# The first piece of w_down in three loads instead of one: 112, 12 and 4 partitions

## The chip, the cores and the metric

The kernel runs on one core of one Trainium2 chip. The metric is the device time of one execution in microseconds (us); the number compared is the median of several runs. A core has five engines that run their own instruction streams: PE (TensorE, matrix multiplications; its weight loads are counted apart as PEld), DVE (VectorE), ACT (ScalarE), POOL (GpSimd) and SP (SyncE, which here only issues loads). Sixteen DMA engines move data between the chip's memory (HBM) and the on-chip buffer of 128 partitions.

## What is computed

One token for each of two batch rows goes through a transformer block with adaptive layer norm: a modulation vector from the condition `c`, attention over a window of cached keys and values, and a gated feed-forward network. Cut to what matters:

```python
mod = (silu(c) @ w_mod).reshape(2, 6, 1, 640)          # sa, ca, ga, sb, cb, gb
h = layernorm(x) * (1 + ca) + sa
q = h @ wq                                             # 32 heads of 192
k, v = k_cache[:, :, -1024:, :], v_cache[:, :, -1024:, :]
o = softmax(q @ k.T * 192**-0.5) @ v
x = x + ga * (o.reshape(2, 1, 6144) @ wo)
h = layernorm(x) * (1 + cb) + sb
x = x + gb * ((gelu(h @ w_gate) * (h @ w_up)) @ w_down)   # 640 -> 1536 -> 640
```

All inputs are bf16. `w_down` has 1536 x 640 elements.

## The kernel before

Everything that is large comes from HBM once, by loads that SP issues: w_mod, wq, the nine pieces of the keys and values, wo, w_gate, w_up and w_down, in this order, 76.9 MB in all. They land in one large buffer, `arena` (L194), whose places are used again: the table `place` (L198 to L215) says at which columns each piece stands, and its order is the order of issue. The function `pump` (L333) issues the next loads as far as the pieces that stood in the same columns have been consumed; SP then waits for PE's counter where it must. All loads are issued by the line L290 (`k_dma`), so it is one line in the profile. Each load has a semaphore of its own (`sem_of`, L286), which is raised sixteen times in all while it lands, and whoever reads the piece waits for 16.

The kernel keeps track of who writes and reads what by keys: a piece is cut into units of 128 columns, each one key (`keys`, L300), and `_Sched` (L29) works out from them which waits an instruction needs.

w_down is laid out with 12 rows of the matrix on each partition, (p r) n -> p (r n), and comes as three pieces, `WD_SPLIT` (L172): the rows 0 to 7 of each partition, 10,240 B a partition (1280 KB in all), then the rows 8 to 10 (480 KB), then row 11 (160 KB). `source` (L311) gives the place in HBM and `view` (L306) the place in `arena`; both take all 128 partitions. They are the last three loads of the kernel.

On the compute side, DVE multiplies a piece of the keys by the query (L512), PE sums it over groups (L524), DVE sums the rest (L531); the softmax follows (L536 to L555), and PE multiplies the weights with the values (L575). After the last values come the output projection (L634), the second layer norm, w_gate and w_up (L655), and the product of both halves, which DVE transposes to `aT` (L669). Then PE multiplies by w_down in three groups of matmuls (L677), one for each piece of `WD_SPLIT`: 64, 24 and 8 matmuls, all added up in one PSUM bank. Each group waits for `aT` and for its own piece. Two DVE steps (L683, L685) and the store on ACT's queue (L687) end the kernel. ACT's queue also loads `c` (2 rows) and x (8 rows) at the start (L346, L347). PE fills its waits with matmuls whose result is not used (`keep_clock`).

Of the kernel before, what the change touches and what calls it, by code (L numbers as in the profile page):

```python
# [119 lines left out]
def bass_adaLN_cond__sliding_block_cached__geglu_ffn__decode_kernel(  # L120
# [14 lines left out]
    P = 128  # L135
    B, _, D = A_x.shape
    _, H, Sk, Dh = A_k_cache.shape
# [12 lines left out]
    FC = F // P  # L150
# [13 lines left out]
    UNIT = 128  # L164
# [5 lines left out]
    WO_SPLIT = [(0, NT)]  # L170
    WU_SPLIT = [(0, KT)]
    WD_SPLIT = [(0, 8), (8, 3), (11, 1)]  # L172
    RB = 16
    RM = RB * (B - 1) + 1
    SB = RB // 2
    OC = DR // 2
    GM = SB + 1
    OM = RB + SB + 1
    ZW = P + DD - 1
# [8 lines left out]
    with es:  # L188
        S = _Sched(nc, es)
# [4 lines left out]
        arena = sb("arena", [P, NAR], BF16)  # L194
# [3 lines left out]
        place = {("wm", 0): (0, KT * 6 * D), ("wq", 0): (4 * HS, wq_n[0])}  # L198
        tiles = [("k", 0, 0, 10), ("k", 0, 1, 12), ("k", 0, 2, 0), ("v", 0, 0, 5), ("k", 1, 0, 9), ("v", 0, 1, 0), ("k", 1, 1, 5), ("v", 1, 0, 9), ("v", 1, 1, 0)]
        span = {}  # L200
        for kind, b, t, z in tiles:
            j0, n = (K_SPLIT if kind == "k" else V_SPLIT)[b][t]
# [7 lines left out]
        o_d = o_u + KT * F  # L210
        place[("wg", 0)] = (o_g, KT * F)
        for i, (k0, nk) in enumerate(WU_SPLIT):
            place[("wu", i)] = (o_u + k0 * F, nk * F)
        for i, (r0, nr) in enumerate(WD_SPLIT):
            place[("wd", i)] = (o_d + r0 * D, nr * D)  # L215
        assert all(o % UNIT == 0 and n % UNIT == 0 and o + n <= NAR for o, n in place.values())
        wm_v = arena[:, 0:KT * 6 * D].rearrange("p (k n) -> p k n", k=KT)
        wg_v = arena[:, o_g:o_g + KT * F].rearrange("p (k n) -> p k n", k=KT)
# [46 lines left out]
        aR = sb("aR", [P, FT], BF16)  # L265
        aT = sb("aT", [P, RB + FC * 32], BF16)
        halfsel = sb("halfsel", [P, 2], F32)
# [8 lines left out]
        BK_OT = 6  # L276
# [4 lines left out]
        def bank(k):  # L281
            return ("bank", k)

        sem_x = S.sem("d_x")
        sem_c = S.sem("d_c")
        sem_of = {it: S.sem("d_%s" % "_".join(str(z) for z in it)) for it in place}  # L286
        sem_out = S.sem("d_out")

        def k_dma(dst, src):
            return lambda e: e.dma_start(dst, src)  # L290
# [3 lines left out]
        queue = {"next": 0, "done": set(), "ops": {}}  # L294

        def overlap(x, y):
            (a, m), (b, n) = place[x], place[y]
            return a < b + n and b < a + m

        def keys(it, lo=0, width=None):  # L300
            o, n = place[it]
            width = n - lo if width is None else width
            assert lo + width <= n
            return [("ar", z) for z in range((o + lo) // UNIT, -(-(o + lo + width) // UNIT))]

        def view(it, lo=0, width=None):  # L306
            o, n = place[it]
            width = n - lo if width is None else width
            return arena[:, o + lo:o + lo + width]

        def source(it):  # L311
            kind = it[0]
            if kind == "wm":
                return w_mod.rearrange("(p k) n -> p (k n)", k=KT)
            if kind == "wq":
                k0, n = WQ_SPLIT[it[1]]
                return A_wq.rearrange("(p k) n -> p (k n)", k=KT)[:, k0 * NQ:(k0 + n) * NQ]
            if kind == "wo":
                t0, n = WO_SPLIT[it[1]]
                return A_wo.rearrange("(p t) n -> p (t n)", t=NT)[:, t0 * D:(t0 + n) * D]  # L320
            if kind == "wg":
                return B_w_gate.rearrange("(p k) n -> p (k n)", k=KT)
            if kind == "wu":
                k0, nk = WU_SPLIT[it[1]]
                return B_w_up.rearrange("(p k) n -> p (k n)", k=KT)[:, k0 * F:(k0 + nk) * F]
            if kind == "wd":
                r0, nr = WD_SPLIT[it[1]]
                return B_w_down.rearrange("(p r) n -> p (r n)", r=FC)[:, r0 * D:(r0 + nr) * D]
            b, (j0, n) = it[1], span[it]
            src = A_k_cache if kind == "k" else A_v_cache  # L330
            return src[b][:, K0:Sk, :].rearrange("h (x j) d -> h x j d", x=XQ)[:, :, j0:j0 + n, :].rearrange("h x j d -> h x (j d)")

        def pump(*consumed):  # L333
            queue["done"].update(consumed)
            while queue["next"] < len(items):
                n = queue["next"]
                it = items[n]
                if not all(x in queue["done"] for x in items[:n] if overlap(x, it)):
                    break
                queue["ops"][it] = S.dma("sp", k_dma(view(it), source(it)), sem_of[it], writes=keys(it), name="ld_%s" % "_".join(str(z) for z in it))  # L340
                queue["next"] += 1

        pump()
        wm_dma = queue["ops"][("wm", 0)]
        S.op("pool", lambda e: e.memset(xr[:, :], 0.0), writes=["xr"], name="xr0")
        S.dma("act", k_dma(crow[:, :], c[:, :]), sem_c, writes=["crow"], name="ld_c")  # L346
        S.dma("act", k_dma(xr[0:P:RB, :], A_x[:, 0, :].rearrange("b (i n) -> i b n", i=NR)), sem_x, writes=["xr"], name="ld_x")  # L347
        S.op("pool", lambda e: e.memset(epsc[:, 0:1], 0.0), writes=["epsc"], name="epsc0")
        S.op("pool", lambda e: e.memset(epsc[:, 1:2], EPS), reads=["epsc"], writes=["epsc"], name="epsc1")
        for nm, t in (("scT", scT), ("oT", oT)):  # L350
# [6 lines left out]
             reads=["ones_f"], writes=["ident_f"], name="ident_f")  # L357
        S.op("pool", lambda e: e.tensor_copy(out=ident_b[:, :], in_=ident_f[:, :]),
             reads=["ident_f"], writes=["ident_b"], name="ident_b")
        S.op("pool", lambda e: e.memset(aT[:, 0:RB], 0.0), writes=["aT0"], name="aT0")  # L360
        S.op("pool", lambda e: e.memset(selq[:, :, :], 0.0), writes=["selq"], name="selq0")
        for b in range(B):
# [4 lines left out]
                 reads=["ones_b"], writes=[("selt", b)], name="selt%d" % b)  # L367
            S.op("pool", lambda e, b=b: e.tensor_copy(out=selq[:, b, :].rearrange("p (u x) -> p u x", x=SQW)[:, :, 0:P].rearrange("p u (i v) -> p u i v", i=NR)[:, :, :, 0:XQ],
                                                      in_=selt[:, b, :].rearrange("p (i x) -> p i x", x=XQ).unsqueeze(1).broadcast_to([P, HB, NR, XQ])),
                 reads=[("selt", b), "selq"], writes=["selq"], name="selq%d" % b)  # L370
        S.op("pool", lambda e: e.memset(scl[:, :], SCALE), writes=["scl"], name="scl")
        S.op("pool", lambda e: e.memset(zsel[:, :, :], 0.0), writes=["zsel"], name="zsel0")
        for i in range(2):
            S.op("pool", lambda e, i=i: e.affine_select(out=zsel[:, :, :], in_=zsel[:, :, :], pattern=[[-P, 2], [-1, ZW]],
                                                        compare_op=ALU.not_equal, fill=1.0, base=DD - 1 - 2 * P * i, channel_multiplier=DD),
                 reads=["zsel"], writes=["zsel"], name="zsel%d" % (i + 1))
# [4 lines left out]
             reads=["ident_f"], writes=["mask_h"], name="mask_h")  # L381
        S.op("dve", lambda e: e.tensor_reduce(out=st32[:, :], in_=ident_f[:, :].rearrange("p (i m) -> p m i", m=32), axis=AX.X, op=ALU.add),
             reads=["ident_f"], writes=["st32"], name="st32")
        S.op("dve", lambda e: e.tensor_reduce(out=halfsel[:, :], in_=st32[:, :].rearrange("p (h m) -> p h m", h=2), axis=AX.X, op=ALU.add),
             reads=["st32"], writes=["halfsel"], name="halfsel")
# [3 lines left out]
             reads=["st32"], writes=["selstat"], name="selstat")  # L389
# [3 lines left out]
        def c_T(e):  # L393
            last = None
            for j in range(KT):
# [4 lines left out]
             reads=[bank(BK_T)], writes=["scT"], name="silu")  # L400
        S.op("dve", lambda e: e.tensor_copy(out=X[:, :], in_=xr[:, :]),  # L401
             reads=["xr"], writes=["X"], name="x_f32")
# [26 lines left out]
        def ln_mod(tag, opc_idx, s_idx, dst_bf):  # L429
# [15 lines left out]
             reads=["mask_h"], writes=["maskc"], name="maskc")  # L445
        S.op("dve", lambda e: e.tensor_copy(out=maskE[:, :], in_=mask_h[:, :]), reads=["mask_h"], writes=["maskE"], name="maskE")

        for half in range(2):
            def f(e, half=half):
                last = None  # L450
                for k in range(KT):
# [9 lines left out]
                 reads=[bank(half)], writes=[("modR", half)], name="mod%d_evac" % half)  # L461
            S.op("dve", lambda e, half=half: e.tensor_scalar(out=opc[:, half, :], in0=modR[:, 3 * half + 1, :], scalar1=1.0, scalar2=None, op0=ALU.add),  # L462
                 reads=[("modR", half)], writes=[("opc", half)], name="opc%d" % half)
# [27 lines left out]
        for n in range(NQB):  # L491
            if n % 2 == 0:
                S.op("act", lambda e, n=n: e.activation(out=qrow[:, n * QW:(n + 1) * QW], in_=ps[:, n, :], func=ACTF.Copy),  # L493
                     reads=[bank(n)], writes=[("qrow", n)], name="q1_evac%d" % n)
            else:
                S.op("dve", lambda e, n=n: e.tensor_copy(out=qrow[:, n * QW:(n + 1) * QW], in_=ps[:, n, :]),  # L496
                     reads=[bank(n)], writes=[("qrow", n)], name="q1_evac%d" % n)
        for b in range(B):
            def f(e, b=b):
                last = None  # L500
                for u in range(HB):
# [5 lines left out]
                 reads=[bank(BK_T + b)], writes=[("qbc", b)], name="q2_evac%d" % b)  # L507
# [78 lines left out]
        for n, it in enumerate(tiles):  # L586
            kind, b, t = it
# [7 lines left out]
            j0, w = span[it]  # L595
# [16 lines left out]
        def p_sel(e):  # L612
            last = None
            for dd in range(DD):
# [10 lines left out]
             reads=[bank(BK_OT), "oT"], writes=["oT"], name="oT")  # L625
# [3 lines left out]
        def wo_f(e):  # L629
            last = None  # L630
            wv = view(("wo", 0)).rearrange("p (t i n) -> p t i n", t=NT, i=NR)
            for t in range(NT):
# [9 lines left out]
             reads=[bank(2), ("modR", 0)], writes=["lnt"], name="ga_attn")  # L642
        S.op("dve", lambda e: e.tensor_tensor(out=X[:, :], in0=lnt[:, :], in1=X[:, :], op=ALU.add),
             reads=["lnt", "X"], writes=["X"], name="x1")
# [4 lines left out]
        def ffn_gu(bk, wv, name, splits):  # L649
            for ci, (k0, nk, key) in enumerate(splits):  # L650
# [12 lines left out]
             reads=[bank(0)], writes=["gl"], name="gelu")  # L663
# [4 lines left out]
             reads=[bank(1), "gl"], writes=["aR"], name="geglu")  # L668
        S.op("dve", lambda e: e.transpose(aT[:, RB:RB + FC * 32], aR[:, :]), reads=["aR"], writes=["aT"], name="aT")  # L669
        for ci, (r0, nr) in enumerate(WD_SPLIT):  # L670
            def f(e, r0=r0, nr=nr):
                last = None
                for fc in range(r0, r0 + nr):
                    wv = wd_v[:, fc, :].rearrange("p (i h n) -> p i h n", i=NR, h=2)
                    for h, a, m in ((1, 0, OM), (0, RB, GM)):
                        for i in range(NR):
                            last = e.matmul(ps[32 * i:32 * i + m, BK_OT, CY:CY + OC], lhsT=aT[:, 32 * fc + a:32 * fc + a + m], rhs=wv[:, i, h, :],  # L677
                                            start=(fc == WD_SPLIT[0][0] and h == 1), stop=(fc == WD_SPLIT[-1][0] and h == 0), tile_position=(0, 32 * i),
                                            skip_group_check=True)
                return last  # L680
            S.op("pe", f, reads=["aT", "aT0"] + keys(("wd", ci)), writes=[bank(BK_OT)], name="down%d" % ci)

        S.op("dve", lambda e: e.tensor_tensor(out=fin[:, :], in0=ps[:, BK_OT, CY:CY + OC], in1=go[:, :], op=ALU.mult),  # L683
             reads=[bank(BK_OT), "go"], writes=["fin"], name="gb_y")
        S.op("dve", lambda e: e.tensor_tensor(out=finb[:, :], in0=fin[:, :], in1=xo[:, :], op=ALU.add),  # L685
             reads=["fin", "xo"], writes=["finb"], name="outR")
        S.dma("act", k_dma(out[:, 0, :].rearrange("b (u n) -> u b n", n=OC), finb[0:P:SB, :]),  # L687
              sem_out, reads=["finb"], name="st_out")
# [17 lines left out]
        for n, x in enumerate(body):  # L706
            if x.opcode != "Matmult":
                continue
            w = x.ins[1]
# [37 lines left out]
```

## Time and profile before

| | us |
|---|---|
| median of 3 runs | 185.89 (185.77 to 185.96) |
| the profiled execution | 185.71 |
| its span, first to last instruction | 184.5 |
| read from HBM | 76.88 MB, 417 GB/s over the span |
| w_up, issue to landing | 23.0 |
| w_down, first, second, third piece, issue to landing | 25.8, 26.4, 26.4 |
| last load issued | 155.4 |
| first, second, third group of w_down's matmuls start | 180.39, 181.43, 181.84 |

The profile is of one execution. It gives the busy time of each engine, the span in 40 equal slices (each digit is a busy share in tenths), the DMA queues (q1 is SP's, q10 ACT's; q8 and q14 carry instructions and tables), the chain of waits that ended last (each line: start, length, what), groups of instructions by source line, and a timeline. The busy times count no instructions that only wait or issue. Behind these views the trace has a record of each DMA packet (queue, start, length, bytes, but not which of the sixteen engines) and the time of each semaphore increment.

### The profile page before, as it was taken

The numbers are of one execution on the slowest core, as the hardware profiler recorded it, in microseconds if no ns is written. First come the engines' busy times: TensorE is split into PE (matmuls) and PEld (weight loads), VectorE is DVE, ScalarE is ACT, GpSimd is POOL, SyncE is SP. The second block draws the span as 40 slices with busy tenths as digits, with TensorE's granted clock in tenths as the row PEclk, the third lists the DMA queues.
The fourth block names the chain that finished last, engine by engine and source line by source line (L and its number), as shares of the span: only waits on it lengthen the run. The fifth ranks groups of instructions, "written<-read, shape, count | busy, mean of one in ns | idle before, by whom it ended". The sixth has DMA issues, their size and how long they took to land.

```text
span 184.5 us, 1871 instructions
## 1 busy us (share of the span) xinstructions
PE 107.9 (59%) x967; PEld 28.2 (15%) x695; DVE 107.2 (58%) x105; ACT 14.4 (8%) x27; POOL 6.1 (3%) x23
## 2 busy tenths in 40 slices
PE   0017000966665095653599565957663299898783
PEld 0012000130000000002351000600000266405212
DVE  6022200039994499964991999587995658300631
ACT  2042000042000000001000000010000100320410
POOL 8400000000000000000000000000000000000000
PEclk9999755599999669997569999988999579999999
DMA  8999997999898989899999989898989999989991
GB/s 292 492 483 440 426 426 330 448 442 494 368 490 362 501 352 512 362 481 416 437 458 409 469 373 480 384 480 373 490 373 480 426 453 470 426 340 400 418 393 46
DMA packets 2495, 76.99 MB, mean 417 GB/s; under 512 B 310, under 2 KB 440, under 8 KB 568
## 3 DMA queue, kind: packets, MB, share of 16 engines
q1 hardware_dynamic: 2448, 76.87, 97.1%
q8 instruction: 6, 0.10, 0.2%
q10 hardware_dynamic: 40, 0.01, 0.0%
q14 instruction: 1, 0.01, 0.0%
HBM read 76.88 MB, written 0.00 MB: 417 GB/s over the span
## 4 chain that ended last, share of the span: by engine, by line
DMA 58%; DVE 22%; PE 17%; ACT 1%; issue 1%; SPq 0%
DMA arena<-in_A_k_cache_dram 36%; DMA arena<-in_B_w_down_dram 14%; DVE arena L512 12%; PE ps L575 8%; DMA arena<-in_w_mod_dram 8%; DVE S_sb L531 6%; PE ps L524 5%; DVE Em L561 2%; PE ps L454 2%; DVE negm L541 1%; ACT E_sb L549 1%; PE ps L552 1%; PE ps L545 1%; DVE M L537 0%; SPq L290 0%
## 5 line engine op out<-in xcount | busy, mean ns | idle before, releaser
L524 PE MATMUL ps<-arena,ident_b 128*128 128x512 bf16 x192 | 49.3, 400 | 28.4 <-DVE arena L512 28.3
L512 DVE TENSOR_TENSOR arena<-arena,qbc 128x3072 bf16<-128x3072 bf16 x32 | 54.8, 1750 | 9.2 <-DMA arena<-in_A_k_cache_dram 7.5
L575 PE MATMUL ps<-arena,Em 128*64 128x384 bf16 x256 | 25.5, 367 | 5.6 <-DVE Em L561 5.6
L531 DVE TENSOR_REDUCE S_sb<-ps 128x32 f32<-128x1024 f32 x16 | 19.5, 1219 | 8.5 <-PE ps L524 8.5
L575 PEld LDWEIGHTS ps<-arena,Em 128*64 128x64 bf16 x256 | 15.9, 124 | 30.4 <-DVE Em L561 22.2
L561 DVE TENSOR_TENSOR Em<-E_sb,maskE 128x2048 bf16<-128x2048 bf16 x8 | 18.0, 2283 | 2.3 <-PE ps L575 2.3
L486 PE MATMUL ps<-arena,hT 128*2 128x512 bf16 x60 | 5.9, 573 | 14.7 <-DMA arena<-in_A_wq_dram 14.7
L496 DVE CAST qrow<-ps 128x512 bf16<-128x512 f32 x1 | 0.7, 691 | 18.7 <-PE ps L486 18.7
L408 PE MATMUL ps<-Em,ident_b 128*128 128x512 bf16 x48 | 11.2, 379 | 0.4 <-issue 0.3
L539 PEld LDWEIGHTS ps<-ident_f,M 128*1 128x1 f32 x2 | 0.2, 80 | 61.0 <-DVE M L537 61.0
L641 DVE TENSOR_TENSOR lnt<-ps,modR 128x160 f32<-128x160 f32 x1 | 0.3, 325 | 12.9 <-PE ps L634 12.9
L549 ACT ACTIVATE E_sb<-S_sb,nbias 128x256 bf16<-128x256 f32 x2 | 1.0, 508 | 66.3 <-DVE nbias L547 66.3
L582 ACT ACTIVATE On<-ps,rden 128x384 bf16<-128x384 f32 x2 | 1.2, 580 | 48.6 <-PE ps L575 48.6
L454 PE MATMUL ps<-arena,scT 128*17 128x480 bf16 x40 | 3.5, 523 | 1.9 <-DMA arena<-in_w_mod_dram 1.9
L634 PEld LDWEIGHTS ps<-arena,oT 128*17 128x17 bf16 x192 | 3.3, 91 | 7.6 <-DMA arena<-in_A_wo_dram 7.6
L396 PE MATMUL ps<-ident_b,crow 2*128 2x2 bf16 x5 | 0.4, 177 | 6.6 <-DMA crow<-in_c_dram 6.6
L634 PE MATMUL ps<-arena,oT 128*17 128x160 bf16 x192 | 3.5, 233 | 0.8 <-DMA arena<-in_A_wo_dram 0.8
L417 PE MATMUL ps<-st,selstat 128*128 128x2 f32 x4 | 0.9, 298 | 4.9 <-ACT sqj L413 4.9
L401 DVE CAST X<-xr 128x160 f32<-128x160 bf16 x1 | 0.2, 244 | 6.0 <-DMA xr<-in_A_x_dram 6.0
L486 PEld LDWEIGHTS ps<-arena,hT 128*2 128x2 bf16 x20 | 0.7, 118 | 19.2 <-issue 19.2
L462 DVE TENSOR_SCALAR opc<-modR 128x160 f32<-128x160 f32 x2 | 0.4, 223 | 4.1 <-ACT modR L459 4.1
L493 ACT ACTIVATE qrow<-ps 128x512 bf16<-128x512 f32 x2 | 1.1, 594 | 19.9 <-PE ps L486 19.9
(86 smaller groups left out, 51.4 us busy)
## 6 DMA issues: line engine op xcount, KB each, us to landing
arena<-in_A_v_cache_dram SPq DMA_DIRECT2D x4, 6144.0 KB, 26.5
arena<-in_A_k_cache_dram SPq DMA_DIRECT2D x3, 6144.0 KB, 36.9
arena<-in_A_wq_dram SPq DMA_DIRECT2D x1, 7680.0 KB, 31.5
arena<-in_A_wo_dram SPq DMA_DIRECT2D x1, 7680.0 KB, 27.7
arena<-in_A_k_cache_dram SPq DMA_DIRECT2D x2, 3072.0 KB, 42.3
arena<-in_w_mod_dram SPq DMA_DIRECT2D x1, 4800.0 KB, 14.2
arena<-in_B_w_gate_dram SPq DMA_DIRECT2D x1, 1920.0 KB, 21.0
arena<-in_B_w_up_dram SPq DMA_DIRECT2D x1, 1920.0 KB, 23.0
```

The source lines that it names most:

```text
L408: last = e.matmul(ps[:, BK_T, :], lhsT=ident_b[:, :], rhs=Em[:, 0, 0:512 // H, :].rearrange("p j h -> p (j h)"), start=True, stop=True)
L454: last = e.matmul(ps[32 * i:32 * i + RM, half, 0:MH].rearrange("p (m n) -> p m n", n=DR), lhsT=scT[:, k, :], rhs=wv[:, 3 * half:3 * half + ...
L486: last = e.matmul(ps[32 * i:32 * i + B, n, :], lhsT=hT[:, k, 0:RM:RB], rhs=wv[:, kk, i, n * QW:(n + 1) * QW], start=(k == 0), stop=(k == K ...
L512: S.op("dve", lambda e: e.tensor_tensor(out=kt, in0=kt, in1=qbc[:, b, :].unsqueeze(1).broadcast_to([P, JC, Dh]), op=ALU.mult), reads=[("qb ...
L524: last = e.matmul(o_ap, lhsT=ident_b[:, :], rhs=kt[:, :, t * GC:(t + 1) * GC], start=(t == 0), stop=(t == NCH - 1))
L531: S.op("dve", lambda e: e.tensor_reduce(out=S_sb[:, b, 2 * JC * pair:2 * JC * (pair + 1)], in_=ps[:, 2 * z:2 * z + 2, :].rearrange("p k (j ...
L541: S.op("dve", lambda e: e.tensor_reduce(out=negm[:, b, :].rearrange("p (h x) -> p h x", x=XQ), in_=ps[0:1, BK_T, 0:P].rearrange("p (h x) - ...
L545: S.op("pe", lambda e: e.matmul(ps[:, BK_T, P:P + 1], lhsT=negm[:, b, :], rhs=scl[:, :], start=True, stop=True), reads=[("negm", b), "scl" ...
L549: S.op("act", lambda e: e.activation(out=E_sb[:, b, :], in_=S_sb[:, b, :], func=ACTF.Exp, scale=SCALE, bias=nbias[:, b:b + 1], accum_out=d ...
L561: S.op("dve", lambda e, z=z, j=j: e.tensor_tensor(out=Em[:, z, :, :], in0=E_sb[:, b, j:j + JE].unsqueeze(2).broadcast_to([P, JE, H]), in1= ...
L575: last = e.matmul(ps[64 * i:64 * i + 2 * H, BK_O, 0:ON], lhsT=Em[:, z, 2 * jp:2 * jp + 2, :].rearrange("p j h -> p (j h)"), rhs=view(it, l ...
L634: last = e.matmul(ps[32 * i:32 * i + RM, 2, 0:DR], lhsT=oT[:, t, :], rhs=wv[:, t, i, :], start=(t == 0), stop=(t == NT - 1), tile_position ...
```

## The change

The first piece of w_down (1280 KB, 128 partitions of 10,240 B) is no longer one load but three, of the same columns: the partitions 16 to 127, then 0 to 11, then 12 to 15. The description of the change says that the first goes over all DMA engines, the second over three and the third over four. The other two pieces stay as they were, behind them.

`WE_SPLIT` gives the first partition and the number of partitions of each part. The three loads have keys of their own for each part, so that none waits for the other, and share one semaphore; the first group of matmuls reads all three, and so waits for 48 increments. `older` collects whoever used these columns before, since the new keys do not meet the old ones. No wait on SP comes of it. The order of instructions on PE, DVE, ACT and POOL is the same; SP has 17 loads instead of 15.

```diff
--- before.py
+++ after.py
@@ -170,6 +170,8 @@
     WO_SPLIT = [(0, NT)]
     WU_SPLIT = [(0, KT)]
     WD_SPLIT = [(0, 8), (8, 3), (11, 1)]
+    WE_SPLIT = [(16, 112), (0, 12), (12, 4)]
+    assert sorted(WE_SPLIT)[0][0] == 0 and sum(n for _, n in WE_SPLIT) == P
     RB = 16
     RM = RB * (B - 1) + 1
     SB = RB // 2
@@ -211,8 +213,10 @@
         place[("wg", 0)] = (o_g, KT * F)
         for i, (k0, nk) in enumerate(WU_SPLIT):
             place[("wu", i)] = (o_u + k0 * F, nk * F)
+        wd_keys = [[("we", i) for i in range(len(WE_SPLIT))]] + [[("wd", i)] for i in range(1, len(WD_SPLIT))]
         for i, (r0, nr) in enumerate(WD_SPLIT):
-            place[("wd", i)] = (o_d + r0 * D, nr * D)
+            for it in wd_keys[i]:
+                place[it] = (o_d + r0 * D, nr * D)
         assert all(o % UNIT == 0 and n % UNIT == 0 and o + n <= NAR for o, n in place.values())
         wm_v = arena[:, 0:KT * 6 * D].rearrange("p (k n) -> p k n", k=KT)
         wg_v = arena[:, o_g:o_g + KT * F].rearrange("p (k n) -> p k n", k=KT)
@@ -283,7 +287,8 @@
 
         sem_x = S.sem("d_x")
         sem_c = S.sem("d_c")
-        sem_of = {it: S.sem("d_%s" % "_".join(str(z) for z in it)) for it in place}
+        sem_of = {it: S.sem("d_%s" % "_".join(str(z) for z in it)) for it in place if it[0] != "we" or it[1] == 0}
+        sem_of.update({it: sem_of[("we", 0)] for it in wd_keys[0]})
         sem_out = S.sem("d_out")
 
         def k_dma(dst, src):
@@ -295,18 +300,24 @@
 
         def overlap(x, y):
             (a, m), (b, n) = place[x], place[y]
-            return a < b + n and b < a + m
+            return a < b + n and b < a + m and not x[0] == y[0] == "we"
 
         def keys(it, lo=0, width=None):
             o, n = place[it]
             width = n - lo if width is None else width
             assert lo + width <= n
+            if it[0] == "we":
+                return [("ar", z, it[1]) for z in range((o + lo) // UNIT, -(-(o + lo + width) // UNIT))]
             return [("ar", z) for z in range((o + lo) // UNIT, -(-(o + lo + width) // UNIT))]
+
+        def parts(it):
+            return WE_SPLIT[it[1]] if it[0] == "we" else (0, P)
 
         def view(it, lo=0, width=None):
             o, n = place[it]
+            p0, np_ = parts(it)
             width = n - lo if width is None else width
-            return arena[:, o + lo:o + lo + width]
+            return arena[p0:p0 + np_, o + lo:o + lo + width]
 
         def source(it):
             kind = it[0]
@@ -323,9 +334,10 @@
             if kind == "wu":
                 k0, nk = WU_SPLIT[it[1]]
                 return B_w_up.rearrange("(p k) n -> p (k n)", k=KT)[:, k0 * F:(k0 + nk) * F]
-            if kind == "wd":
-                r0, nr = WD_SPLIT[it[1]]
-                return B_w_down.rearrange("(p r) n -> p (r n)", r=FC)[:, r0 * D:(r0 + nr) * D]
+            if kind in ("wd", "we"):
+                r0, nr = WD_SPLIT[it[1] if kind == "wd" else 0]
+                p0, np_ = parts(it)
+                return B_w_down.rearrange("(p r) n -> p (r n)", r=FC)[p0:p0 + np_, r0 * D:(r0 + nr) * D]
             b, (j0, n) = it[1], span[it]
             src = A_k_cache if kind == "k" else A_v_cache
             return src[b][:, K0:Sk, :].rearrange("h (x j) d -> h x j d", x=XQ)[:, :, j0:j0 + n, :].rearrange("h x j d -> h x (j d)")
@@ -337,7 +349,10 @@
                 it = items[n]
                 if not all(x in queue["done"] for x in items[:n] if overlap(x, it)):
                     break
-                queue["ops"][it] = S.dma("sp", k_dma(view(it), source(it)), sem_of[it], writes=keys(it), name="ld_%s" % "_".join(str(z) for z in it))
+                o, w = place[it]
+                older = [S.bufs[z] for z in (("ar", y) for y in range(o // UNIT, (o + w) // UNIT)) if z in S.bufs] if it[0] == "we" else []
+                older = [x[0] for x in older if x[0] is not None] + [y for x in older for y in x[1]]
+                queue["ops"][it] = S.dma("sp", k_dma(view(it), source(it)), sem_of[it], writes=keys(it), deps=older, name="ld_%s" % "_".join(str(z) for z in it))
                 queue["next"] += 1
 
         pump()
@@ -678,7 +693,7 @@
                                             start=(fc == WD_SPLIT[0][0] and h == 1), stop=(fc == WD_SPLIT[-1][0] and h == 0), tile_position=(0, 32 * i),
                                             skip_group_check=True)
                 return last
-            S.op("pe", f, reads=["aT", "aT0"] + keys(("wd", ci)), writes=[bank(BK_OT)], name="down%d" % ci)
+            S.op("pe", f, reads=["aT", "aT0"] + [z for it in wd_keys[ci] for z in keys(it)], writes=[bank(BK_OT)], name="down%d" % ci)
 
         S.op("dve", lambda e: e.tensor_tensor(out=fin[:, :], in0=ps[:, BK_OT, CY:CY + OC], in1=go[:, :], op=ALU.mult),
              reads=[bank(BK_OT), "go"], writes=["fin"], name="gb_y")
```

## The prediction

> **What bounds the kernel now.** I read the busy times first, then the row of DMA shares, then the chain of waits, then its last stretch beside the timeline, and last the trace's records of single packets.
>
> ```profile
> PE 107.9 (59%) x967; PEld 28.2 (15%) x695; DVE 107.2 (58%) x105; ACT 14.4 (8%) x27; POOL 6.1 (3%) x23
> DMA  8999997999898989899999989898989999989991
> DMA packets 2495, 76.99 MB, mean 417 GB/s; under 512 B 310, under 2 KB 440, under 8 KB 568
> q1 hardware_dynamic: 2448, 76.87, 97.1%
> q8 instruction: 6, 0.10, 0.2%
> ```
>
> No engine is busy over 59% of the span, while SP's queue (q1) takes 97.1% of sixteen DMA engines' time. The kernel is one long stream of loads, and it ends when the stream ends. The chain of waits, from 154 us to the end, says the same:
>
> ```profile
> 154.49 0.43 SPq L290
> 154.92 0.04 issue
> 154.96 26.43 DMA arena<-in_B_w_down_dram
> 181.39 0.04 issue
> 181.43 0.40 PE ps L677 x24
> 181.83 0.01 issue
> 181.84 0.28 PE ps L677 x8
> 182.12 0.02 issue
> 182.15 0.25 DVE fin L683
> ```
>
> The long piece is w_down waiting in the queue. The timeline has the consumer's side:
>
> ```profile
> 178.87 0.58 DVE L669 STREAM_TRANSPOSE aT<-aR 128x384 bf16<-128x384 bf16 x1
> 180.39 0.76 PE L677 MATMUL ps<-arena,aT 128*25 128x80 bf16 x64 [0.83 <-DMA arena<-in_B_w_down_dram]
> 181.43 0.66 PE L677 MATMUL ps<-arena,aT 128*25 128x80 bf16 x32 [0.29 <-DMA arena<-in_B_w_down_dram]
> ```
>
> aT is there at 179.45, but the 64 matmuls of the first piece start at 180.39, the 24 of the second at 181.43, the 8 of the third at 181.84: each starts on a landing. Behind the last landing stand 0.28 us of matmuls, two DVE steps and the store. So what the last landing moves, the end moves, one for one.
>
> **Why the last landing is late.** Each load raises its semaphore sixteen times, once for each DMA engine. For the last load these increments came at 179.96, 180.02, 180.04, 180.05, 180.10, 180.19, 180.20, 180.21, then 180.51, 180.69, 181.08, 181.40, 181.63, 181.64, 181.70, 181.80. Eight engines are level; eight are behind by 0.3 to 1.6 us. The packet records say why. On one engine a packet starts 3 to 4 ns before the end of the one ahead of it, so sixteen lanes can be followed through the span (now and then two cross within a nanosecond, and the identity is then a guess). The six instruction packets (q8, 16 KB) began at 43.16, 100.12, 152.25, 163.67, 173.22 and 181.36; the one at 152.25 took 1.072 us, and the row after it 2.764 us where such rows took 2.267. That is 1.57 us lost by one lane, never made up while the queue is full. Five such lanes, one that carried ACT's table load at 78.58 and two that began late are the eight.
>
> **The change, part by part.**
> Removed: one load of 128 rows of 10,240 B, eight rows for each lane. A row took 0.385 to 0.396 us in the records, eight in a row 3.08 (174.967 to 178.047 on one lane), so 0.385 a row.
> Added: 112 rows, seven for each lane: -0.385 us on all sixteen. Then 12 rows over three lanes, four each: +4 x 0.385 = +1.54. Then 4 rows over four, one each: +0.385. Each load also ends with a 4-byte packet of 0.009 us on each lane that it uses.
> Net: three lanes carry 12 rows (+1.54 + 0.02 = +1.56), one carries 8 (+0.01), twelve carry 7 (-0.385).
>
> On SP: two more issues, 2 x 0.43 = 0.87 us, and the two later pieces of w_down are issued 0.87 us later (from about 155.0 and 155.4 to 156.7). Their rows are due at 178. The cover is the queue ahead, wo, w_gate and w_up, 21 to 28 us from issue to landing; without it the cost would be the 0.87. Nothing else stands behind them on SP's queue except its wait for the output. ACT's and POOL's queues are not touched.
> On PE: the first group of 64 matmuls waits for 48 increments where it waited for 16; behind it stand the other 32 and, on DVE, fin. That wait is over no later than those of the pieces behind it in the same lanes, so it costs nothing by itself: 64 matmuls (0.76) must be done when the third piece lands. If they are not, at most that 0.76 is added.
>
> Which lanes get the extra rows is not shown for these shapes. The nearest rows are the two small loads on ACT's queue: c (2 rows) ran on two lanes and x (8 rows) on four, and the two of c were among the four of x (one lane has q10 packets at 4.55, 6.02, 7.44 and 8.87). I take it that a load on few lanes uses the same first ones. Followed to the end, the two lanes of c are level (packets end at about 179.54 and 179.72). Of the other two lanes of x, one ends at 179.74 or, if it was the lane of the fetch at 152.25, at 181.27; the other most likely carried the table load and ends at 180.63, with some chance of 179.65 or 181.19. All lanes' last packet ends at 181.37, and its landing is told at 181.80.
> With +1.56 the two level lanes end at 181.10 and 181.28, below 181.37. The third lane decides: 181.30 if level (end earlier by 0.07), 182.19 after the table load (+0.82), 182.83 after the fetch (+1.46). The other late lanes fall to 180.99 and no longer count. I give the level case somewhat under half, and so the middle of the other two, about +1.0, is my value; both ends, -0.07 and +1.46, stay in the range.
>
> The price of a row is the second unknown: rows of the 128-row loads have always been dealt out in one way, and 112 rows may be dealt so that two lanes write to the same place. Lower bound 0 (a row costs 0.385, as in every row of the records). Upper bound: the only rows here that ran beside a disturbance, those after an instruction packet, took 0.50 us more; on all seven rows that is +3.5. I take 0, the nearer row by kind, and keep the upper bound as a rival.
>
> [...]
>
> **The sum.** The profiled execution took 185.71 us, 184.5 of it the span and 1.2 around it; the median of the runs is 185.89, so 0.18 more. 185.71 + 1.0 = 186.7 for such an execution, 186.9 for the median.
>
> **Rivals.**
> 1. No change: the third lane is level too. For: two of the four lanes surely are. Against: one of the other two carried the table load or worse. 185.89 - 0.07 = 185.8; with twelve lanes for the 12 rows and a late lane among those that keep eight, 185.9.
> 2. Faster: the 12 rows run on more lanes than three and the four latest (181.63 to 181.80) are among those that have only seven rows; the end falls with the next one, at 181.40, or by a whole row: -0.39, so 185.5. With three rows on each of four level lanes it would be the same -0.39. For: the late lanes are a small set. Against: the late lanes would have to be just those that are spared. It decides once all five lanes that met a fetch are spared.
> 3. Slower by far: rows collide. For: dealing 112 rows in sevens is new, and the stream already takes nearly all of the engines' time. Against: packets of every size in the records keep one rate. It decides from 0.05 us a row on seven rows (0.35, more than a row saved); at half of the bound, 0.25 a row, +1.75 on top of -0.07 to +1.0, so 187.6 to 188.6.
> That the change does not do what it says (twelve lanes, not three) is in 1 and 2.
>
> **How the numbers follow.** My forecast, one of the extra rows' lanes late, has 0.38, with 186.7 to 187.4 as its own range; rival 1 has 0.26; rival 2 0.18; rival 3 0.18. A measurement of this kernel can tell about 0.2% from no change, 0.37 us. Faster 0.18 (rival 2), same 0.26 (rival 1), slower 0.56 (forecast and rival 3). The predicted time is 186.9. The range goes from 185.5 (rival 2's value) to 188.3, which leaves out the upper part of rival 3 and a faster case below a whole row: about 0.2 together.
>
> **What would show it.** In the issues by line, five loads of w_down instead of three, the two new ones of 120 and 40 KB. In the increments of the last load: three that come over 1.5 us later against the others than now (right), or one row earlier for a few (twelve lanes). In the records, 10,240 B rows still at 0.385 us; if they take 0.5 or more, rival 3 holds. The 64 matmuls of the first piece still start on a landing, and the three groups close together. The forecast is wrong if the increments draw together, or if another engine than DMA ends the chain.

## The result

The changed kernel takes 190.61 us in the median (189.70 to 190.88, four runs), the one before 185.93 in the same comparison: a ratio of 1.0245, 95% interval 1.023 to 1.026. It is slower by 4.7 us. The forecast was 186.9 with a range of 185.5 to 188.3, so the sign was right, and the size and the range were wrong. The profiled execution, the fastest of the four, took 189.70 us, 188.4 of it the span; before it was 185.71 and 184.5. SP issues 19 loads where it issued 17; the 17 and 15 given with the change are each two too low.

From the page of the changed kernel, busy shares by slice and the queue of SP:

```profile
span 188.4 us, 1873 instructions
DMA  8999999999979989899998999989999999989991
q1 hardware_dynamic: 2464, 76.87, 97.3%
```

At first sight little is different: the same bytes, and a queue as busy as before (97.3% against 97.1%). The row of DMA shares is misleading here, and the stretches at the end show it. First the kernel before, then the changed one; the columns are the stretch, its length, busy time of PE, PEld, DVE, ACT and POOL with the number of instructions, the granted PE clock, the DMA share and GB/s.

```profile
174.60:178.00 3.40, 2.79 (x44) 0.90 (x41) 1.11 (x5) 1.06 (x2) 0.00 (x0) 1.00 0.94 398
178.00:181.40 3.40, 2.16 (x73) 0.74 (x65) 1.14 (x2) 0.00 (x0) 0.00 (x0) 1.00 0.67 262
```

```profile
174.60:178.00 3.40, 2.40 (x27) 0.49 (x21) 1.81 (x8) 1.81 (x3) 0.00 (x0) 1.00 1.04 239
178.00:181.40 3.40, 1.78 (x20) 0.62 (x21) 0.00 (x0) 0.00 (x0) 0.00 (x0) 0.74 0.98 212
181.40:184.80 3.40, 2.37 (x59) 0.53 (x59) 1.14 (x2) 0.00 (x0) 0.00 (x0) 0.76 0.77 183
```

From 174.6 us on, where the first rows of w_down's first piece start, the DMA engines are at least as busy as before and move less: 239 GB/s in place of 398, then 212 at a share of 0.98 in place of 262 at 0.67, where the stream before was already ending. Most packets last longer. The records say it directly (median duration of a packet, and the last landing of w_down, all in us):

| | 10,240 B | 3840 B | 1280 B | last landing |
|---|---|---|---|---|
| before | 0.388 | 0.149 | 0.055 | 181.80 |
| changed | 0.729 | 0.281 | 0.074 | 185.76 |

The chain of waits of the changed kernel (start, length, what):

```profile
155.77 0.33 SPq L295
156.10 0.04 issue
156.14 0.43 SPq L295
156.57 0.04 issue
156.62 0.44 SPq L295
157.06 0.04 issue
157.10 0.25 SPq L295
157.35 0.04 issue
157.39 27.96 DMA arena<-in_B_w_down_dram
185.36 0.04 issue
185.40 0.40 PE ps L692 x24
185.80 0.01 issue
185.81 0.28 PE ps L692 x8
```

It is the same chain as before: a load of w_down is issued, waits in the queue, and its landing releases the last matmuls. The wait itself is only 1.53 us longer (27.96 against 26.43) and begins 2.43 later. The later issue is not what delays the rows: the first row of w_down's first piece starts at 174.63, before it was 174.82. And the consumer's side, from the timeline:

```profile
179.61 1.78 PE L670 MATMUL ps<-arena,h2T 128*9 128x384 bf16 x20 [1.96 <-DMA arena<-in_B_w_up_dram]
182.10 0.58 DVE L684 STREAM_TRANSPOSE aT<-aR 128x384 bf16<-128x384 bf16 x1
184.32 0.76 PE L692 MATMUL ps<-arena,aT 128*25 128x80 bf16 x64 [0.71 <-DMA arena<-in_B_w_down_dram]
185.40 0.66 PE L692 MATMUL ps<-arena,aT 128*25 128x80 bf16 x32 [0.32 <-DMA arena<-in_B_w_down_dram]
```

Even w_up, which the change does not touch, lands later: 179.57 in place of 177.12. A lane here is one of the sixteen DMA engines, followed through the packet records. The level lanes already carry rows of w_down while the late lanes still carry w_up. The 15 rows of w_up that begin after the first row of w_down took 0.681 to 1.469 us each; before, the 14 such rows took 0.573 to 0.582. aT is there at 182.68, still 1.5 us ahead of the last part of the first piece (184.19), so the end is still set by w_down.

### The profile page after: what moved, and what is told of

Read it like the earlier page. It is cut to its first block, busy times and chain, and to the rows that moved or that the text cites. A ratio compares the mean times of both kernels' runs of the same rounds, so it can differ in the third digit from the quotient of the medians.

```text
span 188.4 us, 1873 instructions
## 1 busy us (share of the span) xinstructions
PE 110.5 (59%) x967; PEld 28.5 (15%) x695; DVE 107.4 (57%) x105; ACT 14.4 (8%) x27; POOL 6.1 (3%) x23
## 3 DMA queue, kind: packets, MB, share of 16 engines
q1 hardware_dynamic: 2464, 76.87, 97.3%
## 4 chain that ended last, share of the span: by engine, by line
DMA 58%; DVE 22%; PE 17%; SPq 1%; ACT 1%; issue 1%
DMA arena<-in_A_k_cache_dram 36%; DMA arena<-in_B_w_down_dram 15%; DVE arena L527 12%; PE ps L590 8%; DMA arena<-in_w_mod_dram 7%; DVE S_sb L546 6%; PE ps L539 4%; DVE Em L576 2%; PE ps L469 2%; SPq L295 1%; DVE negm L556 1%; ACT E_sb L564 1%; PE ps L567 1%; PE ps L560 1%; DVE M L552 0%
## 5 line engine op out<-in xcount | busy, mean ns | idle before, releaser
L539 PE MATMUL ps<-arena,ident_b 128*128 128x512 bf16 x192 | 50.1, 404 | 29.6 <-DVE arena L527 29.6
L501 PE MATMUL ps<-arena,hT 128*2 128x512 bf16 x60 | 5.4, 534 | 14.0 <-DMA arena<-in_A_wq_dram 14.0
L423 PE MATMUL ps<-Em,ident_b 128*128 128x512 bf16 x48 | 11.8, 395 | 0.5 <-issue 0.5
L469 PE MATMUL ps<-arena,scT 128*17 128x480 bf16 x40 | 4.2, 602 | 1.8 <-DMA arena<-in_w_mod_dram 1.8
L670 PE MATMUL ps<-arena,h2T 128*9 128x384 bf16 x40 | 2.8, 422 | 2.6 <-DMA arena<-in_B_w_up_dram 2.0
L681 DVE TENSOR_TENSOR aR<-ps,S_sb 128x384 bf16<-128x384 f32 x1 | 0.6, 558 | 5.0 <-PE ps L670 5.0
```

The costliest lines, as they stand in the source:

```text
L423: last = e.matmul(ps[:, BK_T, :], lhsT=ident_b[:, :], rhs=Em[:, 0, 0:512 // H, :].rearrange("p j h -> p (j h)"), start=True, stop=True)
L469: last = e.matmul(ps[32 * i:32 * i + RM, half, 0:MH].rearrange("p (m n) -> p m n", n=DR), lhsT=scT[:, k, :], rhs=wv[:, 3 * half:3 * half + ...
L501: last = e.matmul(ps[32 * i:32 * i + B, n, :], lhsT=hT[:, k, 0:RM:RB], rhs=wv[:, kk, i, n * QW:(n + 1) * QW], start=(k == 0), stop=(k == K ...
L539: last = e.matmul(o_ap, lhsT=ident_b[:, :], rhs=kt[:, :, t * GC:(t + 1) * GC], start=(t == 0), stop=(t == NCH - 1))
L670: last = e.matmul(ps[32 * i:32 * i + GM, bk, 0:FT], lhsT=h2T[:, k, 0:RM:2], rhs=wv[:, k, i * FT:(i + 1) * FT], start=(k == 0), stop=(k == ...
```

## The experiments

The theory at the start, P, is a conjecture of the author: lanes don't meet in the on-chip buffer as long as a load has 128 rows; 112 rows dealt in sevens, and 12 or 4 rows dealt over a few lanes, make lanes meet there, and lanes that meet share one lane's rate. The rivals: the small loads on few lanes cost the time (F, later C), the number of loads and the wait for 48 do, or loads that are not of 128 rows are slow for a reason on the HBM side (H). A later one, L: the change would have worked but for the meeting. Times are medians, ratios against the kernel before on the same chip; row times are medians of the rows of 10,240 B unless another size is named.

**e1_112_16: one part undone.** From the changed kernel:

```diff
-    WE_SPLIT = [(16, 112), (0, 12), (12, 4)]
+    WE_SPLIT = [(16, 112), (0, 16)]
```

> One part of the change alone: 112 partitions, then the other 16 as one load; no load of 12 or 4. [...] Theory F (the few-lane loads of 12 and 4 rows are what costs): rows back at 0.385 us, time within 0.4 us of the kernel before.

190.64 us, ratio 1.026 (1.023 to 1.029); rows of 10,240 B at 0.747 us, the longest 1.011, so the 16 rows of the second load did not take over 1 us each, as P had them do. The time is that of the whole change: it does not need the loads of 12 and 4. F falls in this form. The end of its chain:

```profile
156.44 29.97 DMA arena<-in_B_w_down_dram
186.41 0.04 issue
186.46 0.74 PE ps L692 x32
```

**e2_columns: as many loads, all of 128 partitions.** From the kernel before, in `pump`:

```diff
+                if it == ("wd", 0):
+                    for c0, nc_ in ((0, 3 * D), (3 * D, 3 * D), (6 * D, 2 * D)):
+                        queue["ops"][it] = S.dma("sp", k_dma(view(it, c0, nc_), source(it)[:, c0:c0 + nc_]), sem_of[it], writes=keys(it, c0, nc_), name="ld_wd_0_%d" % c0)
+                    queue["next"] += 1
+                    continue
```

> The first piece in three loads again and one semaphore raised to 48, but each of all 128 partitions, split by columns (3, 3 and 2 of the eight rows of the matrix on a partition: 3840, 3840 and 2560 B). If the number of loads, the shared semaphore or the later issue cost the time, 189 us or more. Theory P: the lanes keep to themselves, the only cost is 2 x 8 short packets for each lane; 185.7 to 186.5 us, rows of 3840 B at 0.15 us.

185.90 us, ratio 1.0014 (1.0002 to 1.0025): 0.26 us for two more loads, later issue and the wait for 48 together. Rows of 3840 B at 0.149 us, last landing at 181.90. The number of loads is not the cause.

**e3_low64 and e4_mid64: the same 64 rows of HBM into two places.** From the kernel before, in `pump`; e4_mid64 has `[32:96, :]` in place of `[0:64, :]` in `view(it)`, the destination. The other half of the piece is not loaded in either:

```diff
+                if it == ("wd", 0):
+                    queue["ops"][it] = S.dma("sp", k_dma(view(it)[0:64, :], source(it)[0:64, :]), sem_of[it], writes=keys(it), name="ld_wd_0")
+                    queue["next"] += 1
+                    continue
```

> Left out: the partitions 64 to 127 of the first piece of w_down are not loaded. The load is of 64 rows into the partitions 0 to 63. [...] Theory H (HBM side, or any load that is not of 128 rows): the same as the run e4_mid64.

> Left out: half of the first piece, as in e3_low64, and the same 64 rows of HBM, but they go into the partitions 32 to 95 (the rows of the matrix stand on the wrong partitions). [...] Theory H: rows as slow as in e3_low64 and the same time.

187.91 us against 184.62: ratios 1.011 (1.003 to 1.020) and 0.994 (0.991 to 0.997). The first is of two runs, 187.26 and 188.57, and lies above the author's estimate by P, 185 to 187 (four rows at twice 0.385 us in place of eight at 0.385); its rows were that slow, but the estimate left out that w_up would be slowed, too (last landing 178.97 in place of 177.12). For e4_mid64 the estimate by P, four rows fewer at a steady 0.385 us, was 184.4 to 184.7 us, and the time lies in it. Rows took 0.763 us (median) on the partitions 0 to 63 and 0.387 on 32 to 95. Source, size and number of rows are the same and only the partitions written differ, so H falls, and so does anything that looks only at the shape. The stretches, first of e3_low64, then of e4_mid64, the last two columns being DMA share and GB/s:

```profile
174.60:176.20 1.60, 0.95 (x18) 0.40 (x20) 1.46 (x7) 1.20 (x1) 0.00 (x0) 1.00 1.17 275
176.20:178.20 2.00, 1.31 (x16) 0.10 (x1) 0.20 (x1) 0.49 (x1) 0.00 (x0) 1.00 0.95 183
```

```profile
174.60:176.20 1.60, 0.95 (x19) 0.32 (x19) 1.50 (x7) 1.32 (x2) 0.00 (x0) 1.00 0.92 379
176.20:178.20 2.00, 2.00 (x32) 0.59 (x25) 0.31 (x2) 0.49 (x1) 0.00 (x0) 1.00 0.90 361
```

From 176.2 us on, DMA engines just as busy (0.95 and 0.90) move half as much: 183 against 361 GB/s. A row of e3_low64 takes 1.97 times as long as one of e4_mid64 (0.763 against 0.387 us), which P reads as lanes that meet two by two in e3_low64 and not at all in e4_mid64. Which rows a lane takes is not in the records, and where lanes would meet was not shown; that the 112 rows meet in the same way is P's reading of rows as slow as these (0.73 to 0.75 us), and was not seen lane by lane. With e4_mid64 the wait for w_down is gone from the end of the chain, and the time falls by 1.06 us where the last landing falls by 1.39 (181.80 to 180.41), since PE then comes last:

```profile
177.66 0.92 PE ps L659 x20
178.57 0.16 issue
178.73 1.24 PE ps L412 x5
179.98 1.05 PE ps L681 x96
181.05 0.25 DVE fin L687
```

**e5_marks: which lane is which.** The kernel before with tiny loads behind the last one:

```diff
+        for n in range(2, 16):
+            S.dma("sp", k_dma(mark[0:n, n * 32:(n + 1) * 32], B_w_down[0:n, 0:32]), sem_mark, writes=[("mark", n)], name="mark%d" % n)
...
```

> The kernel before with fourteen tiny loads behind the last one: of n = 2 to 15 rows of 64 B, into a small buffer that nothing reads. Each lane's number of 64 B packets tells its place in the order of engines (the first lane gets all, the sixteenth none). [...] Theory L (the change would have worked but for collisions): the four spared lanes, places 12 to 15, are among the five latest. Otherwise late lanes lie at places that keep eight rows, and even without collisions the change could save nothing. Time within 0.5 us of the kernel before.

185.76 us in one run. There were 119 packets of 64 B, and the fourteen loads' semaphore rose by 119 landings (and 14 increments at issue). 119 is 2 + 3 + ... + 15, so the loads of 2 to 15 rows, taken together, had a lane for each row; with 12 rows over three lanes it would have been 110. By the number of 64 B packets behind each lane's last row, lanes 0 and 1 carry c, the table load at 78.69 was on lane 3, and the five instruction fetches (q8) before the end were on the lanes 5, 6, 9, 10 and 11. Where lanes cross within a nanosecond a swap can't be excluded, but every way of following them that fits the order of the packets gave these five. The lanes 12 to 15, which the change spares, hold none of the five; two of them (12 and 15) are the ones that began late, 0.8 us behind. Theory L falls as far as this run goes: the lanes of the changed kernel's own execution can't be named.

**e6_112_only and e7_spare: each half of the change alone.** From the kernel before, in `pump`; first e6_112_only, then e7_spare:

```diff
+                if it == ("wd", 0):
+                    queue["ops"][it] = S.dma("sp", k_dma(view(it)[16:128, :], source(it)[16:128, :]), sem_of[it], writes=keys(it), name="ld_wd_0")
+                    queue["next"] += 1
+                    continue
```

```diff
+                if it == ("wd", 1):
+                    for p0, n0 in ((0, 12), (12, 4)):
+                        S.dma("sp", k_dma(arena[p0:p0 + n0, NAR - 8 * D:NAR], source(("wd", 0))[p0:p0 + n0, :]), sem_spare,
...
```

> Left out: the partitions 0 to 15 of the first piece; only the load of 112 rows is left of the three. [...]

> The kernel before with its one load of 128 rows, and behind it the loads of 12 and of 4 rows once more, into columns that nothing reads: the other half of the change alone, with 160 KB more to move. [...] Theory C: the growth is most of the 4.7 us. [...]

e6_112_only took 189.58 us, ratio 1.019 (1.010 to 1.028), rows at 0.753; e7_spare 188.15, ratio 1.012 (1.003 to 1.020), the longest row 1.241 us. Both halves cost. The ends of the two chains, in this order:

```profile
156.43 28.62 DMA arena<-in_B_w_down_dram
185.04 0.04 issue
185.09 0.68 PE ps L681 x32
```

```profile
156.20 27.55 DMA arena<-in_B_w_down_dram
183.75 0.04 issue
183.79 0.76 PE ps L682 x29
```

The last landings of w_down are at 185.44 and 184.16, 3.6 and 2.4 us later than before (181.80). They do not add up to the 4.0 of the whole change; in e7_spare the twelve and four rows come on top of the 128, in the change they are taken out of them. For e6_112_only the author's estimate by P was 188 to 190 us, from rows near the 0.73 us of the changed kernel, and it holds (189.58 us at 0.753). For e7_spare one or two rows more on a lane at 0.385 us would be 0.4 to 0.8 us, an estimate; measured are 2.2 us by the ratio. C is wrong as the main cause, but the small loads are not free.

## Why the prediction was wrong

**Right.** The queue of loads sets the end, one for one: the last landing moved by 3.96 us (181.80 to 185.76), the profiled execution by 3.99. Five of the late lanes were explained rightly by instruction packets (e5_marks). The cover of SP's later issue held (the first row of w_down started at 174.63 in place of 174.82; the 156.7 us in the prediction should read 156.3 by its own 0.87, and nothing rests on it), and the wait for 48 cost no more than the 0.26 us that e2_columns shows for all of that together. Lanes 0 and 1 are level and a table load fell on one of the next two (e5_marks).

**The step that failed: the price of a row.** The prediction gave it 0 to +3.5 us and took 0, "the nearer row by kind". All rows of the trace before were of loads of 128 rows, in which, by P, no two lanes meet, so their steady 0.385 us said nothing of another dealing. What a row costs was then 0.729 us at the median. A lane that was on time and has eight rows of each piece needs 8 x 0.729 + 8 x 0.281 + 8 x 0.074 = 8.67 us for w_down against 8 x 0.388 + 8 x 0.149 + 8 x 0.055 = 4.74, so +3.9. The first landings come to nearly the same: from the first of w_up to the first of the last load it is 8.70 us (175.23 to 183.93) in place of 4.73 (175.23 to 179.96), though whether one lane has both is not in the records.

The end is set by the late lanes, and there the same 3.96 us came by another way. Taking the last landing of each load as that of one late lane, 2.45 us were already lost when w_up was there (177.12 to 179.57), since its last rows ran beside rows of the first piece. The first piece took 4.62 us behind that in place of 3.13, so +1.49. The second took 1.17 (1.14 before) and the third 0.40 (0.41): the last rows of both were as fast as before, 0.149 and 0.055 us. So on the path to the end more than half of the loss fell on w_up, which stands ahead of w_down and has no term in the prediction, not even in rival 3, which counted seven rows of the first piece.

**Three lanes.** The prediction took the description's "12 over three" for its sum and built its +1.0 (it rounded the middle of +0.82 and +1.46, 1.14) on which of the lanes 0 to 2 is late. The semaphore of the first piece rose 34 times: twice at issue (157.19, 157.53, once for each load that uses fewer than sixteen lanes) and 32 landings, 16 + 12 + 4. So twelve lanes got a row each of the load of 12. No run shows the three lanes, and e5_marks, too, has a lane for each row in the loads of 2 to 15 rows taken together (119 landings). The forecast of one overloaded late lane, +0.82 to +1.46, is therefore not what made the kernel slower, and that its sign was right was luck.

**The rivals.** Rival 3 is what happened, with its own sign of rows over 0.5 us, and its upper end was left out of the range. It was priced at half of its bound, +0.25 a row on seven rows; measured was +0.34 a row at the median, and more time on the rows of w_up, which it did not count. Rival 2 needs the late lanes to be the spared ones; in e5_marks the five latest lanes are among those that keep eight rows.

**What stays open.** Whether a late lane could be helped at all. In e3_low64 a row needs 0.763 us, so two lanes at that pace move no more than one lane of e4_mid64 alone (0.387). If the place that a row is written to sets its time, and not the lane that carries it, a row handed to another lane still takes its time there, and the end comes no earlier. This is the author's estimate, worked out from e3_low64 and e4_mid64, and no run moved rows of a late lane while rows kept their 0.385 us. No version was found that beats the kernel before.

## What to carry to other kernels

A busy share of the DMA engines is not a rate (here 239 GB/s at a share of 1.04 and 398 at 0.94): read GB/s and the duration of packets of a known size beside it. Before a load of all 128 partitions is cut by partitions, ask what its rows will take at the partitions they are written to; 64 rows from partition 32 on kept their time (0.387 us), and the same 64 from partition 0 on took twice as long a row (0.763 us). Count what such a load does to the loads ahead of it that are still landing, and not only its own rows (here w_up landed 2.45 us later). Cutting by columns cost 0.26 us for two loads more (e2_columns).

## What the runs showed of the hardware

One load dealt differently slowed another in flight: w_up landed 2.45 us later (177.12 to 179.57) without any change to it. Where the rows of w_down kept their time it did not: it landed at 177.15 in e2_columns and 177.32 in e4_mid64, but at 178.97 in e3_low64 and 179.37 in e6_112_only. The instruction fetch of 16 KB at 152.25 us on the kernel before set one lane back by 1.57 us (1.072 for the packet and 0.497 on the row behind it, 2.764 in place of 2.267), and in e5_marks five lanes collected one fetch each. PE's granted clock in the changed kernel was 1.00 from 178.0 to 179.6, while PE waited for the late w_up, and 0.50 from 179.6 to 181.4, where the 20 matmuls of w_up took 1.78 us; before, they ran at 1.00 and took 0.99. No run here shows why, and it was not on the path to the end.
